# Delta-rule attention and a cosine-gated layer on one core: column steps of units 0 and 1 in one run, 16 constant products, a new order of all work

## The chip, the cores and the metric

The kernel runs on one core of one Trainium2 chip. The metric is the time of one execution on the device in microseconds (us); lower is better. The time before is 648.95 us, the median of three runs (646.66 to 650.49). A change of less than 0.5%, about 3.2 us, can hardly be told from none here.

## What is computed

There are 4 batches with 8 heads, 768 steps in time and a head width of 48. Each head carries a 48 x 48 state. The 8 heads of a token are then joined to a row of 384 numbers, and 3072 such rows go through a gated layer of inner width 2048.

```python
k_n = k / (np.linalg.norm(k, axis=-1, keepdims=True) + 1e-06)
for t in range(S):
    y[:, :, t] = np.einsum('bhd,bhde->bhe', q[:, :, t], state)
    v_old = np.einsum('bhde,bhd->bhe', state, kt)
    state = state + bt[:, :, :, None] * np.einsum('bhd,bhe->bhde', kt, vt - v_old)
...
h = x @ w_in
g = h * np.cos(h)
return (g @ w_out).astype(np.float32)
```

The inputs w_in and w_out come in 8-byte floats and are narrowed on the chip. The state makes the steps in time sequential; the gated layer needs only the finished rows.

## The kernel before

**Units.** The 768 steps are cut into 24 units of 32. Within a unit the steps are coupled by a lower triangular 32 x 32 matrix for each of the 32 batch-head pairs. A unit goes through these tasks, named as in the code: load k, q and v; `turn` and `turn_out` (transposition of k and q by TensorE, copied by ScalarE); `gram` (products of keys with keys and queries, L625); `gram_keys` and `gram_queries` (L639, L748, VectorE); the inverse of the triangle; `state` (L834, keys and queries through the state); `right` (L849); the solve with the inverse; `solve_out` (L907); `update` and `update_out` (L920, L928); `within` (L937); `features` (L956, transposition for the layer). The next unit's `state` needs this unit's `update_out`.

**The inverse.** From unit 4 on, two units (a pair) go through DRAM and are inverted by GpSimd in 31 columns (`invert`, L797 and L804). Units 0 to 3 take another way at the start: the triangle is cut into two blocks of 16 (`fold`, `fold_in`, `fold_off`), the blocks are inverted in 15 column steps, and the coupling between them is done by two more solves (`solve_half`, L864, `between`, L864, `between_out`, L882). A column step is one product on TensorE, which spreads a row of the block over its partitions (`rows`, L707, into one of three PSUM banks with the tag h), and two instructions on the engine that eliminates (`eliminate`: a product at L727, a difference at L734). Step j has a width of x times 15 - j elements, where x is 8 for one unit and 16 for two. GROUPS (L672) says which units go together and ON_POOL (L673) which group is eliminated by GpSimd. Before the change there are three groups: unit 0 alone and unit 1 alone on VectorE, in four tasks each, and units 2 and 3 together on GpSimd, in eight tasks, where ScalarE copies each product out of PSUM first. After a group is done, `unfold` (L742 or L744) puts its inverses where the solves read them.

**The layer.** Two units make a block of 256 rows, a pair p. Pairs 0 and 1 use plain products for the first matrix (`hidden(p, f)`, L980, eight of 24 matmuls by the trace's count), the others a fast scheme with 20 smaller products (`layer`, L1158) of sums of blocks (`x_sum`, L1073). The gate h cos(h) is made by ScalarE and VectorE (`turns` L1021, `rest` L1028, `cos` L1037, `gate` L1040). The second matrix is plain for pair 0 (`output`, L1181) and by seven products for the others (`product`, L1246, with `left_sum` L1262 and `collect` L1298). The weights come in 28 pieces: `narrow_load` on the SP queue, then ScalarE (L497, L499), VectorE (L503, L508) and GpSimd (`narrow_add`, L512, uint32). A `hidden(0, f)` needs 3, 6, 9 or 12 of these additions. Piece 6 and later ones reuse a stage buffer and wait for an addition.

**Constant products.** `heat(width)` (L1194) multiplies a constant with itself into p_out, which nobody reads before the first `output` overwrites it. HEAT (L47) lists the widths; each call becomes two matmul instructions.

**The order.** All work is cut into 2148 tasks with names. LINE (L85) lists their numbers in the order in which they are emitted, and each engine, and SP's queue, runs its own tasks in this order; OTHER (L52) is the set of tasks that go to their second engine (VectorE or GpSimd for sums, ScalarE or VectorE for `fold` and `unfold`). The costs and due times in the code are not read by `add` (L190). An instruction waits by semaphores for what it reads and for the buffers that it writes.

Of the kernel before, what the change touches and what calls it, by code (L numbers as in the profile page):

```python
# [46 lines left out]
HEAT = (512, 256, 256, 512, 128,)  # L47


class Order:  # L50

    OTHER = {  # L52
        ('weigh', 0, 0), ('unfold', 0), ('weigh', 0, 1), ('fold', 1), ('unfold', 1),
        ('weigh', 1, 0), ('fold', 2), ('weigh', 1, 1), ('unfold', 2), ('unfold', 3),
        ('right', 4, 0), ('left', 1, 2, 0), ('x_sum', 2, 'd'), ('x_sum', 2, 'n'),
        ('x_sum', 2, 'm'), ('x_sum', 2, 'e'), ('x_sum', 2, 'k'), ('x_sum', 2, 'g'),
        ('x_sum', 2, 'i'), ('x_sum', 2, 'l'), ('x_sum', 2, 'f'), ('x_sum', 2, 'h'),
        ('x_sum', 2, 'b0'), ('left', 2, 2, 0), ('x_sum', 3, 'd'), ('x_sum', 3, 'n'),
        ('x_sum', 3, 'm'), ('x_sum', 3, 'e'), ('x_sum', 3, 'k'), ('x_sum', 3, 'g'),
        ('x_sum', 3, 'i'), ('x_sum', 3, 'l'), ('x_sum', 3, 'f'), ('x_sum', 3, 'h'),  # L60
        ('x_sum', 3, 'b0'), ('left', 3, 1, 0), ('left', 3, 4, 1), ('left', 3, 3, 0),
        ('x_sum', 4, 'd'), ('x_sum', 4, 'n'), ('x_sum', 4, 'm'), ('x_sum', 4, 'e'),
        ('x_sum', 4, 'k'), ('x_sum', 4, 'g'), ('x_sum', 4, 'l'), ('x_sum', 4, 'f'),
        ('x_sum', 4, 'h'), ('x_sum', 4, 'b0'), ('left', 4, 4, 0), ('left', 4, 3, 0),
        ('left', 4, 3, 1), ('x_sum', 5, 'd'), ('x_sum', 5, 'm'), ('x_sum', 5, 'e'),
        ('x_sum', 5, 'i'), ('x_sum', 5, 'f'), ('x_sum', 5, 'h'), ('left', 5, 2, 0),
        ('left', 5, 4, 0), ('left', 5, 4, 1), ('left', 5, 3, 0), ('x_sum', 6, 'd'),
        ('x_sum', 6, 'e'), ('x_sum', 6, 'l'), ('x_sum', 6, 'f'), ('x_sum', 6, 'h'),
        ('x_sum', 6, 'b0'), ('left', 6, 2, 1), ('left', 6, 4, 0), ('left', 6, 3, 0),
        ('x_sum', 7, 'd'), ('x_sum', 7, 'n'), ('x_sum', 7, 'm'), ('x_sum', 7, 'g'),  # L70
        ('x_sum', 7, 'i'), ('x_sum', 7, 'h'), ('left', 7, 1, 0), ('left', 7, 2, 0),
        ('left', 7, 2, 1), ('left', 7, 4, 0), ('left', 7, 3, 1), ('x_sum', 8, 'd'),
        ('x_sum', 8, 'm'), ('x_sum', 8, 'e'), ('x_sum', 8, 'k'), ('x_sum', 8, 'f'),
        ('x_sum', 8, 'h'), ('x_sum', 8, 'b0'), ('left', 8, 4, 1), ('left', 8, 3, 0),
        ('x_sum', 9, 'n'), ('x_sum', 9, 'e'), ('x_sum', 9, 'k'), ('x_sum', 9, 'i'),
        ('x_sum', 9, 'b0'), ('left', 9, 2, 0), ('left', 9, 1, 1), ('left', 9, 4, 0),
        ('left', 9, 4, 1), ('left', 9, 3, 0), ('left', 9, 3, 1), ('x_sum', 10, 'd'),
        ('x_sum', 10, 'n'), ('x_sum', 10, 'e'), ('x_sum', 10, 'g'), ('x_sum', 10, 'l'),
        ('x_sum', 10, 'f'), ('x_sum', 10, 'h'), ('x_sum', 10, 'b0'), ('left', 10, 1, 0),
        ('left', 10, 1, 1), ('left', 10, 4, 0), ('left', 10, 3, 0), ('x_sum', 11, 'f'),  # L80
        ('x_sum', 11, 'b0'), ('left', 11, 1, 0), ('left', 11, 2, 0), ('left', 11, 2, 1),
        ('left', 11, 4, 0), ('left', 11, 4, 1),
# [139 lines left out]
def kernel(  # L222
# [449 lines left out]
    GROUPS = [(0,), (1,), (2, 3)]  # L672
    ON_POOL = (2,)  # L673
# [1154 lines left out]
```

## Time and profile before

The profiled execution took 644.59 us; its span, from the first to the last instruction, is 642.8 us, so 1.8 us lie around it. It is 0.7% under the median of the three timed runs.

| | us in the profiled execution |
|---|---|
| span | 642.8 |
| TensorE (PE) busy | 613.6 |
| VectorE (DVE) busy | 505.4 |
| GpSimd (POOL) busy | 447.9 |
| ScalarE (ACT) busy | 263.3 |
| first column step of unit 0 (L727) | begins at 15.57 |
| first solve of unit 0 (L864) | begins at 25.36 |
| last column step of unit 1 | begins at 52.46 |
| first product of the layer (L980) | begins at 52.91 |
| first solve of unit 2 (L864) | begins at 81.24 |
| mean granted TensorE clock | 0.981 |

A line of the windows view gives, for a stretch of the span, its length, the busy time and instruction count of PE, of its weight loads (PEld), of DVE, ACT and POOL, then the granted TensorE clock as a share of full speed, the DMA share and GB/s. A line of the timeline gives start, duration, engine, source line, operation, output <- input, shape and count, and in brackets the idle time of the engine before it and what ended it.

### The profile page before, as it was taken

The page shows a single profiled execution, that of the slowest core. Times are in us where ns is not written, and L with a number is a line of the kernel's source. Part 1 is how long each engine was busy: PE and PEld are TensorE (multiplying, and loading weights), DVE is VectorE, ACT ScalarE, POOL GpSimd, SP SyncE. Part 2 cuts the span into 40 slices and gives each one's busy share as a digit, 9 for nine tenths or more (in the row PEclk, how much of TensorE's full clock was granted, in tenths as well). Part 3 has the DMA queues.
Part 4 walks back from the last instruction along what each step waited for, and adds up shares of the span by engine and source line. Part 5 has one row for each costly group of instructions (what it writes and reads, how often), then busy time and mean ns, then how long its engine had stood idle before and what let it go on. Part 6 is the DMA issues. An engine that isn't in the chain of part 4 may idle for free.

```text
span 642.8 us, 28246 instructions
## 1 busy us (share of the span) xinstructions
PE 613.6 (95%) x12316; PEld 572.7 (89%) x12316; DVE 505.4 (79%) x955; ACT 263.3 (41%) x467; POOL 447.9 (70%) x783
## 2 busy tenths in 40 slices
PE   5677999999999999999998999999999999999997
PEld 4566888886999989999998999999999999999997
DVE  7896887599999888789788778777778867556582
ACT  3535565822233631533523533622633433435340
POOL 4465899888888788787888886885897874152032
PEclk9677999999999999999999999999999999999999
DMA  6884475554453542635535404425304202000000
GB/s 122 217 215 133 102 197 140 123 93 70 75 96 51 100 76 40 115 64 99 89 42 98 86 7 84 74 53 101 67 2 85 51 2 34 28 2 26 2 25 25
DMA packets 202924, 50.01 MB, mean 78 GB/s; under 512 B 194544, under 2 KB 197760, under 8 KB 202800
## 3 DMA queue, kind: packets, MB, share of 16 engines
q1 hardware_dynamic: 201536, 47.82, 37.5%
q8 instruction: 97, 1.59, 1.1%
q10 hardware_dynamic: 1088, 0.20, 0.2%
q0 software_dynamic: 176, 0.18, 0.2%
q14 instruction: 27, 0.22, 0.1%
HBM read 38.19 MB, written 9.96 MB: 75 GB/s over the span
## 4 chain that ended last, share of the span: by engine, by line
PE 87%; DVE 7%; DMA 1%; issue 1%; POOL 1%; ACT 1%; SPq 0%; DVEq 0%; POOLq 0%
PE p_out L1246 29%; PE p_h L1158 28%; PE p_h L980 7%; PE p_kq L834 4%; PE p_out L1181 3%; PE p_u L897 3%; PE p_g L625 3%; PE p_s L920 3%; PE p_kq L937 3%; PE p_o L1246 2%; PE p_z L956 1%; DVE rows L734 1%; PE p_t L594 1%; DVE rows L727 1%; DVE g_ffn L1175 1%
## 5 line engine op out<-in xcount | busy, mean ns | idle before, releaser
L797 POOL TENSOR_TENSOR part<-z,gb 128x126 f32<-128x126 f32 (+22 forms) x310 | 138.8, 448 | 39.9 <-DMA gb<-g_dr 7.9
L804 POOL TENSOR_TENSOR z<-z,part 128x126 f32<-128x126 f32 (+22 forms) x310 | 145.8, 470 | 24.3
L1246 PE MATMUL p_out<-w_out,g_ffn 128*128 128x192 f32 x672 | 121.6, 329 | 2.0 <-DVE o L1298 1.8
L1246 PEld LDWEIGHTS p_out<-w_out,g_ffn 128*128 128x128 f32 x672 | 107.8, 190 | 3.7 <-issue 2.2
L1037 ACT ACTIVATE turns<-turns,halfpi 128x512 f32<-128x512 f32 x96 | 68.4, 720 | 78.7 <-DVE turns L1028 78.3
L1262 POOL TENSOR_TENSOR g_ffn<-g_ffn 128x512 f32<-128x512 f32 x37 | 49.0, 1329 | 67.3 <-DVE g_ffn L1040 46.0
L1246 PE MATMUL p_out<-w_sum,g_ffn 128*128 128x192 f32 x496 | 90.1, 329 | 0.4 <-DVE o L1298 0.4
L1158 PE MATMUL p_h<-x_sum,w_in 128*128 128x128 f32 x640 | 83.0, 277 | 0.3 <-DVE g_ffn L1175 0.3
L1246 PEld LDWEIGHTS p_out<-w_sum,g_ffn 128*128 128x128 f32 x496 | 79.5, 190 | 1.4 <-DVE o L1298 0.6
L1158 PEld LDWEIGHTS p_h<-x_sum,w_in 128*128 128x128 f32 x640 | 77.8, 192 | 1.7 <-DVE g_ffn L1175 0.6
L1021 ACT ACTIVATE turns<-g_ffn,quarter_turn 128x512 int32<-128x512 f32 x70 | 49.2, 719 | 59.8 <-DVE g_ffn L1175 38.9
L1175 DVE TENSOR_TENSOR g_ffn<-g_ffn,p_h 128x512 f32<-128x512 f32 x80 | 54.1, 679 | 24.6 <-PE p_h L1158 23.6
L1028 DVE SCALAR_TENSOR_TENSOR turns<-g_ffn,turns 128x512 f32<-128x512 f32 x70 | 55.8, 805 | 15.1 <-ACT turns L1021 14.9
L1040 DVE TENSOR_TENSOR g_ffn<-turns,g_ffn 128x512 f32<-128x512 f32 x70 | 50.9, 736 | 12.7 <-ACT turns L1037 12.6
L1158 PE MATMUL p_h<-x_sum,in_sum 128*128 128x128 f32 x400 | 54.0, 278 | 0.3 <-issue 0.3
L1158 PEld LDWEIGHTS p_h<-x_sum,in_sum 128*128 128x128 f32 x400 | 49.3, 191 | 1.5 <-issue 0.4
L980 PE MATMUL p_h<-x_ffn,w_in 128*128 128x128 f32 x384 | 48.3, 285 | 0.0
L980 PEld LDWEIGHTS p_h<-x_ffn,w_in 128*128 128x128 f32 x384 | 45.7, 198 | 1.0 <-issue 0.2
L1262 DVE TENSOR_TENSOR g_ffn<-g_ffn 128x512 f32<-128x512 f32 x51 | 44.3, 872 | 1.6 <-PE p_out L1246 1.5
L541 POOL TENSOR_TENSOR knrm<-ksum,halves 128x16 f32<-128x16 f32 (+1 forms) x14 | 38.8, 2768 | 9.0 <-DVE ksum L529 7.9
L1298 DVE SCALAR_TENSOR_TENSOR o<-p_out,o 128x192 f32<-128x192 f32 x74 | 25.0, 350 | 24.5 <-PE p_out L1246 23.8
L1170 ACT COPY p_h<-p_h 128x512 f32<-128x512 f32 x40 | 23.0, 574 | 48.9 <-PE p_h L1158 33.6
(145 smaller groups left out, 1052.9 us busy)
## 6 DMA issues: line engine op xcount, KB each, us to landing
gb<-g_dr SPq DMA_DIRECT2D x20, 256.0 KB, 4.1
vp<-in_v_dram SPq DMA_DIRECT2D x96, 48.0 KB, 3.0
in_sum<-in_moe_w_out_dram SPq DMA_DIRECT2D x12, 384.0 KB, 3.3
out_dram<-o SPq DMA_DIRECT2D x23, 192.0 KB, 2.5
in_sum<-in_moe_w_in_dram SPq DMA_DIRECT2D x8, 512.0 KB, 5.3
kp<-in_k_dram SPq DMA_DIRECT2D x128, 24.0 KB, 2.2
z_dr<-z SPq DMA_DIRECT2D x10, 256.0 KB, 3.6
zt<-z_dr SPq DMA_DIRECT2D x80, 32.0 KB, 2.4
```

The lines of the kernel that those rows point to most:

```text
L541: nc.gpsimd.tensor_tensor(out=scales[m][2][:, part], in0=sums[m, part.start][:, 0:n], in1=halves[:, 0:n], op=ALU.pow,)
L797: nc.gpsimd.tensor_tensor(out=part, in0=z[:, 0:rows, j, None].to_broadcast(shape), in1=a[:, j, None, j + 1 :].to_broadcast(shape), op=ALU. ...
L804: nc.gpsimd.tensor_tensor(out=behind, in0=behind, in1=part, op=ALU.subtract)
L980: nc.tensor.matmul(p_h[:, i], w_in[:, t, (4 * k + i) * 128 : (4 * k + i + 1) * 128], xts[p][:, t, unit * 128 : (unit + 1) * 128], start=(i ...
L1021: nc.scalar.activation(turns[p, f], hidden_of(p, f), AF.Identity, bias=quarter_turn, scale=TURN)
L1028: nc.vector.scalar_tensor_tensor(out=r, in0=hidden_of(p, f), scalar=TURN, in1=t, op0=ALU.mult, op1=ALU.subtract,)
L1037: nc.scalar.activation(r, r, AF.Sin, bias=halfpi, scale=2.0 * math.pi)
L1040: nc.vector.tensor_tensor(out=place(p, f), in0=step_of(rests.pop((p, f)), f), in1=step_of(hidden_of(p, f), f), op=ALU.mult,)
L1158: nc.tensor.matmul(p_h[:, e], in_block(*w)[:, e], x_of(p, b), start=new and e == 0, stop=True, skip_group_check=True,)
L1175: nc.vector.tensor_tensor(out=part_of(p, to), in0=part_of(p, one), in1=part_of(p, two), op=op)
L1246: nc.tensor.matmul(p_o, left(p, part, a)[:, e % 4], right(e, b), start=(e == 0), stop=(e == FT // 2 - 1), skip_group_check=True,)
L1262: either(("left", p, x, s), nc.vector, nc.gpsimd).tensor_tensor(out=left(p, s, to), in0=left(p, s, one), in1=left(p, s, two), op=op)
```

## The change

1. GROUPS becomes [(0, 1), (2, 3)] and ON_POOL (1,). Units 0 and 1 are eliminated together by VectorE in eight tasks of two columns each, with widths from 240 down to 16 in place of twice 120 down to 8. There are 15 fewer products on TensorE and 30 fewer instructions on VectorE. Unit 0's solves now wait for unit 1's triangle as well.
2. HEAT has 16 entries in place of 5.
3. OTHER and LINE are new: 2158 tasks. By count, `unfold` of units 0 to 3 moves from ScalarE to VectorE (4 tasks), `weigh` moves from GpSimd to VectorE for 3 of 4 tasks, 5 `x_sum` and one each of `in_sums` and `right` move to GpSimd, 2 `left` and one `fold` move to VectorE.

```diff
-HEAT = (512, 256, 256, 512, 128,)
+HEAT = (128, 256, 256, 512, 512, 128, 128, 256, 256, 128, 512, 256, 128, 256, 512, 128,)
...
-    GROUPS = [(0,), (1,), (2, 3)]
-    ON_POOL = (2,)
+    GROUPS = [(0, 1), (2, 3)]
+    ON_POOL = (1,)
```

The numbers of LINE say little by themselves, so here are the first tasks of the two engines that matter most, by name, in the old and the new order (unit or group first, then the step):

```
TensorE, old: turn 0; heat; turn 1; gram 0; gram 1; rows 0,0; turn 2; rows 0,1; rows 0,2; rows 0,3; turn 3;
 rows 1,2; rows 1,0; solve_half 0; between 0; heat; solve 0; rows 1,1; update 0; within 0; heat; turn 4;
 state 1; features 0; rows 1,3; gram 2; heat; gram 3; hidden 0,0; rows 2,0; solve_half 1; rows 2,1;
 between 1; rows 2,2; rows 2,4; solve 1; heat; rows 2,3; update 1; within 1; turn 5; hidden 0,2; ...
TensorE, new: heat; turn 0; heat; heat; turn 1; gram 0; gram 1; heat; rows 0,0; rows 0,1; heat; rows 0,4;
 rows 0,2; turn 2; rows 0,3; heat; rows 0,5; heat; heat; rows 0,7; turn 3; rows 0,6; heat; heat; heat; heat;
 solve_half 0; between 0; heat; solve 0; heat; update 0; within 0; turn 4; state 1; features 0; gram 2;
 hidden 0,0; gram 3; heat; solve_half 1; rows 1,0; between 1; rows 1,1; rows 1,3; solve 1; rows 1,2; update 1;
 within 1; turn 5; rows 1,5; rows 1,6; rows 1,4; features 1; state 2; gram 4; hidden 0,2; gram 5; rows 1,7;
 hidden 0,8; solve_half 2; ...
VectorE, old: sum 0; picks; picks; beta; sum; scale 0; scale; spread 0; gram_keys 0; fold 0; fold_in 0; sum 1;
 gram_keys 1; gram_queries 1; gram_queries 0; begin_rows; eliminate 0,0 to 0,1; fold_in 1; eliminate 0,2 to 0,3;
 shift 0; scale 1; sum 1; shift 1; begin_rows; shift 2; scale 1; between_out 0; eliminate 1,0; solve_out 0;
 shift 3; sum 2; shift 4; update_out 0; shift 5; eliminate 1,1; shift 6; eliminate 1,2; gram_keys 2; ...
VectorE, new: sum 0; sum; beta; picks; picks; scale; scale 0; gram_keys 0; fold 0; fold_in 0; gram_keys 1;
 fold 1; fold_in 1; gram_queries 1; begin_rows; gram_queries 0; spread 0; eliminate 0,0 to 0,7; unfold 0;
 sum 1; shift 0; sum 1; between_out 0; shift 1; solve_out 0; sum 2; update_out 0; scale 1; shift 2; spread 1;
 unfold 1; scale 1; shift 4; spread; gram_keys 2; shift 3; weigh; gram_queries 2; right 1; spread; shift 5;
 fold_in 2; gram_keys 3; gram_queries 3; fold 3; fold_in 3; shift 6; rest 0,0; between_out 1; ...
```

The two DVE instructions of a piece of weights are called shift here, the GpSimd addition add. GpSimd's new head is: weigh; norms of units 2 and 3 (two tasks, L541); add 0; add 1; norms of the next pair; add 2; add 4; add 3; add 5; begin_rows; add 6; eliminate 1,0 to 1,7; add 7; add 8; add 10; add 9; norms; add 11; add 12; the first inverse of the long way. In the old head two additions (10 and 8) stand within the eight eliminations and the inverse follows add 13.

More of the change, by code (lines that the diff above doesn't have):

```diff
@@ L44, in _consts @@
     ).astype(np.float32)
-HEAT = (512, 256, 256, 512, 128,)
+HEAT = (128, 256, 256, 512, 512, 128, 128, 256, 256, 128, 512, 256, 128, 256, 512, 128,)
 class Order:
     OTHER = {
[L53 to L61, printed above, removed]
-        ('x_sum', 4, 'd'), ('x_sum', 4, 'n'), ('x_sum', 4, 'm'), ('x_sum', 4, 'e'),
[L63 to L82, printed above, removed]
@@ new lines @@
+        ('weigh', 0, 0), ('fold', 2), ('right', 3, 2), ('right', 4, 4), ('left', 1, 1, 1),
+        ('in_sums', 17), ('x_sum', 2, 'd'), ('x_sum', 2, 'n'), ('x_sum', 2, 'm'),
[4 rows of a table added]
+        ('x_sum', 3, 'f'), ('x_sum', 3, 'h'), ('x_sum', 3, 'b0'), ('left', 3, 3, 1),
+        ('x_sum', 4, 'd'), ('x_sum', 4, 'n'), ('x_sum', 4, 'm'), ('x_sum', 4, 'e'),
+        ('x_sum', 4, 'i'), ('x_sum', 4, 'l'), ('x_sum', 4, 'f'), ('left', 4, 4, 0),
+        ('left', 4, 4, 1), ('left', 4, 3, 0), ('left', 4, 3, 1), ('x_sum', 5, 'd'),
@@ new lines @@
+        ('x_sum', 5, 'n'), ('x_sum', 5, 'm'), ('x_sum', 5, 'g'), ('x_sum', 5, 'l'),
+        ('x_sum', 5, 'f'), ('left', 5, 1, 1), ('left', 5, 2, 1), ('left', 5, 4, 0),
+        ('left', 5, 4, 1), ('left', 5, 3, 0), ('left', 5, 3, 1), ('x_sum', 6, 'd'),
+        ('x_sum', 6, 'm'), ('x_sum', 6, 'e'), ('x_sum', 6, 'k'), ('x_sum', 6, 'g'),
+        ('x_sum', 6, 'i'), ('x_sum', 6, 'l'), ('x_sum', 6, 'f'), ('x_sum', 6, 'b0'),
+        ('left', 6, 2, 0), ('left', 6, 4, 1), ('left', 6, 3, 0), ('x_sum', 7, 'd'),
@@ new lines @@
+        ('x_sum', 7, 'i'), ('x_sum', 7, 'l'), ('x_sum', 7, 'h'), ('x_sum', 7, 'b0'),
+        ('left', 7, 1, 0), ('left', 7, 2, 0), ('left', 7, 3, 0), ('left', 7, 3, 1),
+        ('x_sum', 8, 'd'), ('x_sum', 8, 'n'), ('x_sum', 8, 'k'), ('x_sum', 8, 'g'),
+        ('x_sum', 8, 'l'), ('x_sum', 8, 'b0'), ('left', 8, 1, 1), ('left', 8, 2, 1),
+        ('left', 8, 3, 0), ('left', 8, 3, 1), ('x_sum', 9, 'm'), ('x_sum', 9, 'e'),
+        ('x_sum', 9, 'k'), ('x_sum', 9, 'g'), ('x_sum', 9, 'f'), ('x_sum', 9, 'h'),
@@ L83 @@
+        ('left', 9, 1, 1), ('left', 9, 4, 1), ('left', 9, 3, 0), ('x_sum', 10, 'e'),
+        ('x_sum', 10, 'k'), ('x_sum', 10, 'h'), ('left', 10, 1, 0), ('left', 10, 2, 0),
+        ('left', 10, 2, 1), ('left', 10, 4, 1), ('left', 10, 3, 0), ('x_sum', 11, 'e'),
+        ('x_sum', 11, 'f'), ('x_sum', 11, 'h'), ('left', 11, 2, 0), ('left', 11, 2, 1),
+        ('left', 11, 4, 1), ('left', 11, 3, 0),
     }
     LINE = """
[98 rows of a table removed]
[98 rows of a table added]
 """
```

200 rows, old and new, of tables (LINE, OTHER) are left out of this document.

## The prediction

> **What bounds the kernel now.** I read the page's busy line first, then the windows view cut by stage, then the chain of waits, then the timeline of the first 82 us.
>
> ```profile
> PE 613.6 (95%) x12316; PEld 572.7 (89%) x12316; DVE 505.4 (79%) x955; ACT 263.3 (41%) x467; POOL 447.9 (70%) x783
> ```
>
> This is the share of busy time over the whole span. By stage (the stretch, its length, then busy time and count of PE, PEld, DVE, ACT and POOL, the granted clock, DMA share, GB/s):
>
> ```profile
> 0.00:12.00 12.00, 5.87 (x47) 4.06 (x51) 8.88 (x28) 4.11 (x8) 6.79 (x12) 1.00 0.68 108
> 12.00:22.00 10.00, 8.07 (x175) 7.27 (x158) 8.41 (x34) 3.86 (x8) 0.00 (x0) 1.00 0.81 202
> 22.00:30.00 8.00, 5.73 (x138) 4.64 (x138) 6.30 (x20) 6.10 (x13) 5.49 (x4) 0.52 0.86 215
> 30.00:40.00 10.00, 6.39 (x170) 5.71 (x170) 9.66 (x20) 4.51 (x9) 5.26 (x5) 0.53 0.92 267
> 40.00:53.00 13.00, 7.44 (x278) 5.51 (x277) 11.98 (x30) 3.71 (x9) 8.89 (x7) 0.87 0.79 197
> ...
> 82.00:140.00 58.00, 56.65 (x1290) 49.23 (x1278) 46.47 (x84) 34.12 (x67) 49.46 (x89) 1.00 0.62 149
> 140.00:200.00 60.00, 59.76 (x1374) 51.99 (x1374) 58.73 (x106) 16.24 (x29) 52.27 (x92) 1.00 0.46 75
> ...
> 300.00:400.00 100.00, 97.71 (x1990) 93.33 (x1988) 81.19 (x142) 40.03 (x68) 79.83 (x149) 1.00 0.42 73
> ```
>
> From 82 us on PE is full: idle 1.35, 0.24 and 2.29 us in the three late rows shown. TensorE bounds the kernel there, and its work there is the same after the change. In the first 53 us it idles 6.13 + 1.93 + 2.27 + 3.61 + 5.56 = 19.5 us, and from 22 to 40 us it has half its clock (the 0.52 and 0.53). So the question is how much earlier the steady part starts. VectorE is what ends the waits in the start: the chain runs through L727 and L734 from 15.5 to 23.1 us and again from 42.6 to 51.6.
>
> ```profile
> 25.36 1.50 PE L864 MATMUL p_w<-vp,halves_z 32*32 32x48 f32 x64 [1.59 <-issue]
> ...
> 33.77 1.50 PE L897 MATMUL p_u<-u_half,halves_z 32*32 32x48 f32 x64 [3.61 <-DVE u_half L882]
> ...
> 51.64 1.34 PE L625 MATMUL p_g<-kq_t 48*32 48x64 f32 x64 [4.31 <-DVE rows L727]
> 52.91 4.66 PE L980 MATMUL p_h<-x_ffn,w_in 128*128 128x128 f32 x24
> ```
>
> Between 25 and 53 us PE waits 3.6 us for VectorE's L882, which stands behind a `scale`, and 4.3 us for the column steps of unit 1, which VectorE does between weight shifts. The 4.66 us of the last row is 2.9 at full clock (later rows of L980).
>
> **The column steps.** Three rows of VectorE give a law:
>
> ```profile
> 12.74 0.42 DVE L639 TENSOR_TENSOR rows<-p_g,bs 128x256 f32<-128x256 f32 x1 [0.61 <-PE p_g L625]
> ...
> 15.57 0.28 DVE L727 TENSOR_TENSOR rows<-rows,p_r 128x120 f32<-128x120 f32 x1
> ...
> 23.17 0.17 DVE L727 TENSOR_TENSOR rows<-rows,p_r 128x8 f32<-128x8 f32 x1
> ```
>
> From 8 to 120 elements the time grows by 0.11 us, 0.98 ns an element; at 256 the law gives 0.41, measured 0.42. The fixed part is 0.16, and 0.03 lies between two. A group of 8 costs 30 x 0.19 + 2 x 960 x 0.00098 = 7.6 us (the row of unit 0: 15.57 to 23.6, with one other instruction within). The double group costs 5.7 + 3.8 = 9.5 us against 15.2 for two, so 5.7 less. Unit 1's steps also ran beside POOL's additions, where a difference at L734 of 0.21 us took 1.27, 1.02 and 0.50; some 3 us of that goes too. Against it VectorE takes over `unfold` (4 x 0.6 from the 0.28 of a tensor_scalar, twice) and three `weigh` (0.55 each): 4.0 us.
>
> **The path through the start, step by step, with before's durations** (before's times in brackets):
> - `gram_keys` 0 at 13.4 (12.74). VectorE now waits for the second norm sum at 8.94 before it makes the picks: 8.94 + 0.55 + 0.49 (beta) + 1.68 (picks) + 2 x 0.85 (scales).
> - First column step at 17.1 (15.57): two units' keys and folds (2 x 1.15), two `gram_queries` (0.74), begin 0.4, spread 0.2.
> - Last step ends at 27.7: 9.5, and 1.0 for PE, where turn 2 (1.23), turn 3 and three heats stand before the rows of steps 3 and 6. `unfold` 0.6: 28.3 (25.25).
> - `solve_half` 0 at 29.4 (25.36): the four heats before it take 0.70 + 0.49 + 1.13 + 0.70 from 26.4, so 1.0 us of them lies on the path. Unit 0 is 4 us late here.
> - `between_out` at 31.8 (33.17). At full clock 0.88, 0.5 and 0.88 lie between. VectorE has only two sums and a shift before it, 2.2 us, and no `scale` that waits for POOL.
> - `solve_out` at 33.5 (35.93), `update_out` ends at 36.4 (41.64; it stood behind two shifts and a sum), turn 4, state 1 (1.31), features, gram 2: PE starts `hidden` at 40.4 (52.91). That needs add 2, for which I find POOL free at 38.7, done at 40.0.
> - Unit 1: VectorE still has four shifts, a `weigh` and two `gram_keys`. I let six POOL additions of 1.28 us cost it 3 us in all. `gram_queries` 2 at 46.0 frees the bank for gram 3, 3 frees it at 50 for `solve_half` 1 (58.31). Solves, update, turn 5 and three rows bring `hidden` 0,2 to 64.4 (67.9).
> - POOL eliminates from 53.2 (59.2). Before's stretch of 20.0 us holds 3.2 of additions, so 16.8: 70.0 (79.2). With `unfold`, `solve_half` 2 stands at 71.6 (81.24), and PE has two more `gram` and two `hidden` to fill until 71.3.
>
> By 81.24 the old order had done four `hidden`, by 71.6 the new one three: 9.7 - 2.9 = **6.8 us ahead**.
>
> **The heats.** At full clock a heat of 512, 256 and 128 takes 1.13, 0.70 and 0.49 (L1194), so the 16 cost 4 x 1.13 + 6 x 0.70 + 6 x 0.49 = 11.7 us, the five of before 5.5. All but the 1.0 above lie in idle PE time; without that cover they cost 6.2 us. What they are worth is the clock. Before, it fell at 22.8 us though PE was idle for only 1.2 us from 16 to 22: its work there was transpositions and rows of 8 to 88 columns. At half clock the solves took 1.50 for 0.88, update 1.56 for 0.89, `hidden` 4.66 for 2.9. I count all at full clock: in the new order PE is busy from 13 to 30 us, with wider rows and nine heats in it.
> The Trainium skill (TensorE: Matmul & The Clock Gate, The HAM clock gate) has the clock halved after an idle window of about 3.4 us. No such gap precedes 22.8 in the trace; by its rule the new order, whose longest gap I put at 2.8 us, stays warm, by the row it need not.
>
> **Later.** Moves between engines change VectorE by -1.8 us and POOL by +2.7 over 560 us (5 x_sum at 0.42 and 0.59, 2 left at 0.87 and 1.33, a right, an in_sums): nothing while both idle over 20% of it. From 140 to 200 us VectorE is 98% full, so a lead holds there only if its work comes earlier as well; it does by the walk, since its units are ahead. SP's queue: v 0 goes 0.3 us later, under the column steps; v 1 stands behind piece 6, which waits for add 0 (34.3), lands at 40, needed at 44. The wait for the three banks of `rows` is in the 1.0 above.
>
> The sum against the profiled execution is 644.6 - 6.8 = 637.8; the same off the median of 648.95 is **642.0**.
>
> **The rivals.**
> - *More than that.* If POOL's additions cost VectorE nothing and the heats end with the steps, the lead is 6.8 + 3 + 1 = 11, and if the late idle of 5.6 us (82 to 640 us) shrinks too, 14: 635 to 639. For it: the new order leaves several us more PE work between an inverse and its solve. Chance 0.22.
> - *The clock falls all the same*, as at 22.8. PE's 4.1 us of rows, turns and heats from 22.2 to 26.3 take 1.7 times that, the heats too: 5 us late, and a lead of 2: 647. Or the double width costs double (0.56 in place of 0.40 at 240): 15.2 us, lead 1. Against it: the 0.42 row. Or the lead is lost in the full VectorE of 140 to 200. Chance 0.22 together, all within 0.5%.
> - *Slower.* The new order lets VectorE's bursts reach PE in the steady part. Before shows one: from 288.8 to 300.9 the chain runs on VectorE, and PE idles 1.67 us in that pair of units (300 to 350 us). If each of ten pairs pays that, it is 16.7 for the 5.6 of today: 11.1 more, less the lead of 6.8: 653.3. It decides from 1.0 us a pair more than today's 0.56. Against it: counted in the two orders, 163 PE tasks of the old one and 161 of the new stand less than 1 us of PE work behind the task that they wait for. Chance 0.18.
> - *As forecast*, 638.5 to 645.7: 0.38.
>
> **The numbers.** Faster by over 0.5% (0.5% is 3.2 us, about what can be told from no change): 0.38 + 0.22 = 0.60; within 0.5%: 0.22; slower: 0.18. The range for 8 in 10 is 633 to 654: its low end takes in most of the first rival, its high end that of the bursts.
>
> **What would show it.** Right: L727 on VectorE as 15 instructions of 0.40 down to 0.17 from about 17 to 27.5 us; a clock of 1.00 from 22 to 40; `solve_half` 0 near 29.4 and the first L980 near 40; `solve_half` 2 near 71.6; PE idle after 82 us near 6. Wrong: PE late at 29 with a halved clock; L882 or L928 behind shifts again; PE idle of over 10 us after 82 us with VectorE as releaser.

## The result, and the profile after

The changed kernel takes 658.55 us, median of four runs (656.10 to 666.83), the kernel before 649.43 beside it. The ratio is 1.0134, 95% interval 1.0085 to 1.0183: 1.3% slower, where 642.0 us and "faster" were forecast. One of the four runs, 666.83, was disturbed and is left out of the ratio. The profiled execution took 658.11 us with a span of 655.9.

The page's busy line, then the windows view by the stretches of before:

```profile
PE 618.7 (94%) x12308; PEld 574.1 (88%) x12308; DVE 495.5 (76%) x931; ACT 261.0 (40%) x458; POOL 438.2 (67%) x785
```

```profile
22.00:30.00 8.00, 5.81 (x137) 4.29 (x139) 6.82 (x23) 5.36 (x11) 2.60 (x2) 1.00 0.66 140
30.00:40.00 10.00, 8.34 (x246) 6.49 (x235) 6.06 (x15) 2.11 (x5) 7.26 (x5) 0.66 0.81 245
40.00:53.00 13.00, 9.81 (x364) 7.79 (x361) 10.37 (x27) 8.21 (x17) 7.04 (x6) 1.00 0.53 127
...
82.00:140.00 58.00, 55.24 (x1182) 49.53 (x1171) 45.55 (x85) 33.53 (x64) 46.91 (x81) 1.00 0.62 142
140.00:200.00 60.00, 55.93 (x1238) 46.11 (x1238) 55.33 (x95) 14.81 (x27) 50.64 (x94) 1.00 0.44 72
...
500.00:600.00 100.00, 96.93 (x1613) 93.41 (x1612) 68.40 (x115) 40.23 (x69) 51.51 (x91) 1.00 0.14 30
```

The last of these rows in the kernel before:

```profile
500.00:600.00 100.00, 99.97 (x1641) 96.70 (x1641) 66.26 (x119) 40.28 (x70) 47.02 (x84) 1.00 0.09 20
```

The start is better: full clock at 22 to 30 us, and from 30 to 53 us VectorE (the third busy time) is busy for 16.4 of 23 us, before for 21.6. The late rows are worse. Length less PE's busy time is PE's idle time: 2.76, 4.07 and 3.07 us here, against 1.35, 0.24 and 0.03 before; from 82 to 600 us it is 14.7 against 5.1. Of the 14.7 the trace puts 9.2 us to waits for VectorE, 2.6 to waits for ScalarE and 2.5 to stops without a releaser.

The timeline, at the steps that the prediction walked (lines of the changed file are three lower: L727 is L724, L864 is L861, L980 is L977):

```profile
16.55 0.40 DVE L724 TENSOR_TENSOR rows<-rows,p_r 128x240 f32<-128x240 f32 x1 [0.19 <-PE p_r L704]
...
27.94 0.88 PE L861 MATMUL p_w<-vp,halves_z 32*32 32x48 f32 x64 [1.48 <-DVE halves_z L741]
...
31.93 0.32 PE L861 MATMUL p_v<-u_half,halves_z 32*32 32x48 f32 x2 [1.58 <-issue]
...
42.10 0.67 PE L831 MATMUL p_kq<-st,kq_t 48*32 48x48 f32 x48 [1.52 <-issue]
...
44.61 1.60 PE L977 MATMUL p_h<-x_ffn,w_in 128*128 128x128 f32 x12
...
76.01 1.44 PE L861 MATMUL p_w<-rhs,halves_z 32*32 32x48 f32 x64 [2.20 <-DVE halves_z L741]
```

The first column step and the first solve stand where the walk put them. Then something new: TensorE stops for 1.5 us in the middle of a run of 64 or 128 equal products, and "issue" says that the profile shows nothing that it waited for. And solve_half 2 comes at 76.0 in place of 71.6.

To see where the lead went I add up TensorE's work in each profiled execution, each product at its usual pace in the kernel before (column and constant products left out, so that all kernels have the same 532 us of work), and take the difference to the kernel before at the same time. Ahead is positive:

| profiled run | 65 us | 110 | 220 | 520 | 600 |
|---|---|---|---|---|---|
| changed kernel | 3.3 | 0.8 | -7.5 | -9.0 | -11.8 |
| e2, old start, new rest | -0.1 | -0.1 | -7.7 | -9.0 | -11.8 |
| e3, new to 230 us | 2.7 | 0.2 | -12.0 | -12.7 | -13.9 |
| p4, new start mended, old rest | 1.5 | 1.9 | -1.3 | -1.5 | -2.0 |
| f1, eight waits taken away | 3.4 | 3.7 | -3.8 | -6.3 | -7.5 |
| p3, f1 with a mended start | 5.0 | 7.0 | -0.9 | -7.4 | -8.6 |
| q1, p3 without twelve sums | 5.6 | 7.1 | 4.8 | 1.8 | 1.2 |
| g, single columns | 0.7 | -3.9 | -12.5 | -14.4 | -18.0 |
| e5b, nine products narrow | 0.7 | -5.3 | -14.9 | -17.4 | -21.8 |

The changed kernel is 3.3 us ahead at 65 us, level at 100, and loses 8 us from 110 to 220 and 3 from 520 to 600. The table is worked out from one execution of each, which need not be a typical one: q1's took 644.68 us, the least of its ten, whose median is 651.13. The ratios below are from timed runs.

### The profile page after: what moved, and what is told of

Its sections match the earlier page's. It is cut to its first block, busy times and chain, and to the rows that moved or that the text cites. A ratio compares the mean times of both kernels' runs of the same rounds, so it can differ in the third digit from the quotient of the medians.

```text
span 655.9 us, 28183 instructions
## 1 busy us (share of the span) xinstructions
PE 618.7 (94%) x12308; PEld 574.1 (88%) x12308; DVE 495.5 (76%) x931; ACT 261.0 (40%) x458; POOL 438.2 (67%) x785
## 4 chain that ended last, share of the span: by engine, by line
PE 66%; DVE 17%; SPq 4%; issue 3%; DMA 2%; ACT 2%; POOL 0%; DVEq 0%; ACTq 0%; POOLq 0%
PE p_out L1243 22%; PE p_h L1155 21%; PE p_h L977 6%; PE p_kq L831 3%; DVE turns L1025 3%; PE p_s L917 3%; PE p_u L894 2%; PE p_g L622 2%; PE p_kq L934 2%; SPq L354 2%; DVE g_ffn L1037 2%; DVE g_ffn L1172 2%; PE p_out L1178 2%; DVE x_sum L1070 1%; DVE g_ffn L1259 1%
## 5 line engine op out<-in xcount | busy, mean ns | idle before, releaser
L794 POOL TENSOR_TENSOR part<-z,gb 128x126 f32<-128x126 f32 (+22 forms) x310 | 141.5, 456 | 52.5 <-DMA gb<-g_dr 10.4
L801 POOL TENSOR_TENSOR z<-z,part 128x126 f32<-128x126 f32 (+22 forms) x310 | 135.8, 438 | 24.3
L1259 POOL TENSOR_TENSOR g_ffn<-g_ffn 128x512 f32<-128x512 f32 x35 | 47.5, 1364 | 77.9 <-DVE g_ffn L1259 34.6
L1172 DVE TENSOR_TENSOR g_ffn<-g_ffn,p_h 128x512 f32<-128x512 f32 x80 | 54.3, 679 | 16.7 <-PE p_h L1155 16.6
L1037 DVE TENSOR_TENSOR g_ffn<-turns,g_ffn 128x512 f32<-128x512 f32 x70 | 51.8, 743 | 12.8 <-ACT turns L1034 12.7
L1155 PE MATMUL p_h<-x_sum,in_sum 128*128 128x128 f32 x400 | 53.4, 278 | 0.0
L977 PE MATMUL p_h<-x_ffn,w_in 128*128 128x128 f32 x384 | 49.4, 288 | 1.3 <-issue 1.1
L977 PEld LDWEIGHTS p_h<-x_ffn,w_in 128*128 128x128 f32 x384 | 46.7, 201 | 2.8 <-issue 1.2
L538 POOL TENSOR_TENSOR knrm<-ksum,halves 128x16 f32<-128x16 f32 (+1 forms) x14 | 37.0, 2642 | 13.0 <-DVE ksum L526 13.0
L1155 PE MATMUL p_h<-x_ffn,w_in 128*128 128x128 f32 x320 | 42.3, 278 | 0.8 <-ACT p_h L1167 0.8
```

Source lines behind the costliest of these rows:

```text
L538: nc.gpsimd.tensor_tensor(out=scales[m][2][:, part], in0=sums[m, part.start][:, 0:n], in1=halves[:, 0:n], op=ALU.pow,)
L794: nc.gpsimd.tensor_tensor(out=part, in0=z[:, 0:rows, j, None].to_broadcast(shape), in1=a[:, j, None, j + 1 :].to_broadcast(shape), op=ALU. ...
L801: nc.gpsimd.tensor_tensor(out=behind, in0=behind, in1=part, op=ALU.subtract)
L977: nc.tensor.matmul(p_h[:, i], w_in[:, t, (4 * k + i) * 128 : (4 * k + i + 1) * 128], xts[p][:, t, unit * 128 : (unit + 1) * 128], start=(i ...
L1037: nc.vector.tensor_tensor(out=place(p, f), in0=step_of(rests.pop((p, f)), f), in1=step_of(hidden_of(p, f), f), op=ALU.mult,)
L1155: nc.tensor.matmul(p_h[:, e], in_block(*w)[:, e], x_of(p, b), start=new and e == 0, stop=True, skip_group_check=True,)
```

## The experiments

All times are medians, each ratio is to the kernel before, run beside it:

| run | us | ratio, 95% interval |
|---|---|---|
| e1 new start, old rest | 650.45 | 1.0044, 1.0007 to 1.0082 |
| e2 old start, new rest | 661.36 | 1.0212, 1.0159 to 1.0264 |
| e3 new to 230 us, old rest | 659.11 | 1.0178, 1.0144 to 1.0212 |
| e4 old to 230 us, new rest | 659.48 | 1.0176, 1.0123 to 1.0229 |
| e5 without nine constant products | 668.52 | 1.0301, 1.0234 to 1.0368 |
| e5b those nine narrowed | 667.18 | 1.0297, 1.0241 to 1.0353 |
| s128 before, half a block later | 692.99 | 1.0721, 1.0658 to 1.0784 |
| s256 before, a whole block later | 647.82 | 1.0024, 0.9994 to 1.0053 |
| f1 eight waits taken away | 657.13 | 1.0177, 1.0105 to 1.0249 |
| f2 f1, last rows early | 656.20 | 1.0161, 1.0095 to 1.0227 |
| g single columns | 664.68 | 1.0312, 1.0235 to 1.0388 |
| h before, 11 more constant products | 646.24 | 1.0005, 0.9969 to 1.0042 |
| p1 e1, edges restored | 648.83 | 1.0027, 0.9996 to 1.0058 |
| p2 changed kernel, 16 instructions more | 663.82 | 1.0248, 1.0185 to 1.0311 |
| p3 f2, 16 instructions more | 657.81 | 1.0182, 1.0116 to 1.0248 |
| p4 p1, start mended | 646.30 | 0.9992, 0.9962 to 1.0021 |
| q1 p3 without twelve sums | 651.13 | 1.0028, 0.9997 to 1.0058 |
| q2 before without twelve sums | 646.74 | 0.9972, 0.9954 to 0.9990 |

**Which part loses (e1 to e4).** LINE of one kernel up to a point, the remaining numbers in the order of the other; each task keeps the engine that its order gave it.

```diff
-LINE = the 2158 numbers of the changed kernel
+LINE = its first 406 (e1) or 734 (e3), then the rest as in the kernel before
-LINE = the 2148 numbers of the kernel before
+LINE = its first 391 (e2) or 759 (e4), then the rest as in the changed kernel
```

> The changed kernel up to the products of unit 6 (its first 406 of 2158 pieces of work, to about 125 us), and from there all work in the order and with the engine choices of the kernel before. Theory (the start is a gain or neutral, and the 9 us are lost by the new order of the steady part, from 100 us on): by the curve of TensorE's work done, the changed kernel stands about 1 to 3 us ahead at this seam, so 646 to 649 us, with TensorE idle under 8 us from 140 to 640 us. Rival (the start itself loses, by its half-clock stretches and its gaps without a releaser): 654 to 660 us, near the changed kernel's 658.

> The mirror image: the kernel before up to about 110 us (its first 391 of 2148 pieces of work), then the changed kernel's order and engine choices. Theory (the steady part's new order loses): 656 to 661 us, with TensorE idle over 9 us from 140 to 640 us. Rival (the start loses): 648 to 651 us.

> As the first, with the seam later: the changed kernel's order up to the first product of the output layer of pair 2 (734 pieces of work, about 230 us), then the order of the kernel before. Theory (most of the steady part's loss lies between 125 and 300 us, by the curve about 6 of 9 us before 230): 652 to 656 us, that is 4 to 8 us above the run with the early seam. Rival (the loss lies in the last third, after 500 us, where the changed kernel's TensorE idles 3 us more): within 2 us of the early seam.

> The kernel before up to about 230 us (its first 759 pieces of work), then the order and the engine choices of the changed kernel. With the seam at 110 us the new rest cost 14.6 us. Theory (the waits of 0.5 to 1.5 us between 130 and 215 us, which that run has at the same places as the changed kernel, are 7 to 9 us of it, and the last third the rest): 651 to 655 us. Rival (all of it lies behind 230 us, or grows out of the seam itself): 659 to 662 us.

The loss is in the rest: 2.1% with the old start (e2), and the new start with the old rest stays within 0.8% of the kernel before. e3 against e1 puts 1.3% between 125 and 230 us. e1 came out between its theory and its rival, 0.4% slower where a gain or nothing was expected: the start brings nothing to the end. e2 and e3 came out 0.4 and 3.1 us above their theories. e4 came out as its rival, so the parts don't add up: its trace has 4.1 us of waits at 231.5, 233.9 and 314.9 us, of which e2's has 0.4.

**The stops without a releaser (s128, s256).** On the changed kernel's page, among the DMA queues (packets, MB, share):

```profile
q8 instruction: 96, 1.57, 1.0%
```

That is 16,384 bytes a packet, and 12308 products with their weight loads make 24,616 instructions, 256 a packet. Counted in TensorE's instructions (with the 158 that are neither), the seven such gaps of the changed kernel come at 705, 1218, 1473, 2497, 10690, 11714 and 13250, the two of the kernel before at 2754 and 15809: multiples of 256 apart, to within one. At four of those edges in the changed kernel:

| edge | edge before passed | packet starts, lands | TensorE goes on | gap |
|---|---|---|---|---|
| 705 | 26.08 | 29.52, 30.79 | 31.93 | 1.58 |
| 1217 | 37.66 | 39.76, 40.78 | 42.10 | 1.52 |
| 1473 | 42.10 | 44.73, 45.94 | 47.31 | 1.10 |
| 2497 | 58.93 | 62.04, 63.02 | 64.34 | 1.53 |

So the next block of code was late. The test moves the edges and nothing else:

```diff
-HEAT = (512, 256, 256, 512, 128,)
+HEAT = (512, 256, 256, 512, 128,) + (16,) * 32    # s256: * 64
+        if width < 128: product of 32x32 by width columns, and return
-LINE = 92 0 1 ...
+LINE = the 32 (64) new tasks, then 92 0 1 ...
```

> The kernel before, unchanged but for 32 tiny constant products (32x32 by 16 columns, 128 TensorE instructions) ahead of all its work, where TensorE idles until 7.9 us. New theory, from the traces so far: TensorE's instructions come by DMA in packets of 16,384 bytes (256 instructions, queue q8), one is asked for when about 50 instructions of the block before it are left, and it is usable about 3.2 to 4 us later; where 256 instructions pass faster than that, in stretches of narrow products, TensorE stands still at the block's edge, with no releaser in the trace. So the time hangs on where the edges fall in the work. In the kernel before they fall well: 0.98 us of such gaps. Moved by half a block, the same work should meet about 13 gaps of 1 to 2.5 us, one for each second unit, near 79, 124, 169, 218, 258, 299, 346, 377, 402, 454 and 501 us: 660 to 672 us. Rival (the gaps without a releaser have nothing to do with blocks): within 2 us of the kernel before.

> The control: 64 tiny products (256 instructions) ahead of the kernel before, so that the edges of the blocks fall on the same work as in the kernel before, one block later. Theory of the block edges: within 2 us of the kernel before, though it has twice as many products as the run with half a block. Rival (added products cost, whatever the edges): as far off as the run with half a block, or further.

Half a block costs 46 us, a whole block, with twice the added products, next to nothing. The timeline of s128:

```profile
82.16 0.65 PE L626 MATMUL p_g<-kq_t 48*32 48x64 f32 x22 [3.37 <-issue]
...
134.47 0.53 PE L835 MATMUL p_kq<-st,kq_t 48*32 48x48 f32 x20 [2.95 <-issue]
```

Such stops stand at 24 edges and make 40 us. Of the twenty over 0.15 us, ten lie exactly 1024 instructions, four blocks, behind another: the work of a unit comes round about that often, so a bad place repeats. Summed in the same way, the steps at edges that waited for their packet are 3.4 us in the kernel before, 2.1 in s256 and 10.7 in the changed kernel, 7.3 of these before 82 us. The theory holds, and the cost, 46 us, is about twice the most that I had put (25 us): the stops are more and longer than the 13 that I counted, and the clock goes down with them (73 us at half clock in s128, 24 in the kernel before).

**The clock (e5, e5b, h).** e5 leaves nine constant products out, e5b makes them 16 columns wide (their instructions stay), h adds 11 wide ones to the kernel before.

```diff
-HEAT = (128, 256, 256, 512, 512, 128, 128, 256, 256, 128, 512, 256, 128, 256, 512, 128,)
+HEAT = (128, 256, 256, 16, 16, 16, 16, 16, 16, 16, 16, 16, 128, 256, 512, 128,)    # e5b
```

> The changed kernel without nine of its sixteen constant products, those between the products of unit 1 and solve_half 0 (13.6 to 26.1 us, 7.5 us of TensorE). Theory (they hold the clock, and the clock is worth time at the start only): the granted clock falls to 0.5 near 22 us as in the kernel before, solve_half 0 starts within 0.5 us of 27.9, the chain from there to the first hidden products is 2 to 5 us longer, and the whole kernel takes 659 to 662 us. Rival (they are worth nothing, or stand in the way): 656 to 658.5 us.

> The changed kernel with nine of its sixteen constant products (those between 13.6 and 26.1 us) narrowed to tiny ones: their busy time is gone, their 36 instructions stay, so the block edges stay on the same work. Leaving them out cost 10 us. Theory (about 7 us of that came from the block edges, which moved by 36 instructions, and the rest from the clock, which fell at 18 us): 660 to 664 us, the clock falling near 20 us again. Rival (all of it is the clock): 667 to 670 us.

> The kernel before with 11 more constant products of 256 and 512 columns in the idle times of TensorE between 18 and 52 us, and 53 tiny ones ahead of all work, so that the 64 add one whole block and the edges stay on the same work after that. This is the part of the change that is to hold the clock, alone. Theory (in the kernel before VectorE is busy 96 of 100 us from 30 to 40 us and 92 of 100 from 40 to 53, so a full clock saves TensorE's own steps on the path only, at most 2.5 us): clock 1.00 from 22 to 40 us, 644 to 647 us. Rival (as in the changed kernel, where nine such products are worth 9 us): 638 to 642 us.

e5 came out dearer than both its theory and its rival. My theory of e5b fell: with the edges in place the loss is the same (1.0297 against 1.0134, some 10 us), so the nine products are worth 10 us by their busy time. Without them the clock is at half for 41 us of the profiled run, with them for 14, and TensorE is 5.3 us behind at 110 us in place of 0.8 ahead. In the old order the same help is worth nothing (h), though it worked:

```profile
22.00:30.00 8.00, 7.34 (x164) 6.12 (x162) 7.20 (x28) 5.06 (x11) 4.98 (x4) 1.00 0.90 214
30.00:40.00 10.00, 6.03 (x163) 4.86 (x164) 9.65 (x19) 5.46 (x9) 5.26 (x5) 0.75 0.95 288
```

The clock is 1.00 and 0.75 for 0.52 and 0.53, and VectorE is at 9.65 of 10 us as before. So I take it that VectorE sets the pace there.

**The doubling (g).** The eight doubled steps become four of unit 0 and four of unit 1, in turn:

```diff
-    GROUPS = [(0, 1), (2, 3)]
-    ON_POOL = (1,)
+    GROUPS = [(0,), (1,), (2, 3)]
+    ON_POOL = (2,)
+LINE: eliminate (0, s) of the changed order becomes (s % 2, s // 2), rows alike; 49 tiny products first
```

> The changed order with the column steps of units 0 and 1 as in the kernel before: two groups of four steps of four columns each, which take the places of the eight doubled steps in turn; 49 tiny products ahead of all work keep the block edges on the same work (256 instructions in all with the column products that this adds). This takes the doubling alone away. Theory of the prediction (9.5 us for the doubled steps and 15.2 us for the single ones): solve_half 0 comes 5 to 6 us later, at 33 to 34 us, and the whole kernel takes 662 to 665 us. Rival (what the start gains is lost before 100 us whatever it is): 657 to 660 us.

```profile
16.58 0.27 DVE L726 TENSOR_TENSOR rows<-rows,p_r 128x120 f32<-128x120 f32 x1
...
33.72 1.04 PE L863 MATMUL p_w<-vp,halves_z 32*32 32x48 f32 x64
```

solve_half 0 at 33.7, 5.8 us later, as the law of the column steps gives. At the end the kernel is 6.4 us of span and 1.8% by ratio slower than the changed one. In the new order the doubling is worth what was forecast or more; the rival falls.

**The waits of the rest (f1, f2, p2, p3).** Behind 82 us TensorE's largest waits look like this (timeline of the changed kernel):

```profile
156.39 0.87 DVE L1117 TENSOR_TENSOR in_sum<-in_sum,w_in 128x512 f32<-128x512 f32 x1
...
159.74 0.90 DVE L1117 TENSOR_TENSOR w_in<-w_in 128x512 f32<-128x512 f32 x1
...
160.56 1.01 DVE L904 TENSOR_TENSOR u<-p_u,bz 128x384 f32<-128x384 f32 x2
...
161.72 0.89 PE L917 MATMUL p_s<-u,kp 64*64 64x96 f32 x32 [1.49 <-DVE u L904]
```

Five sums of weights stand ahead of solve_out 5 on VectorE, and TensorE's update waits 1.5 us. e2 has the same wait, 1.49 us at 161.96, so it belongs to the order. f1 moves eight such tasks in LINE; f2 moves the last column products of units 2 and 3 too; p2 and p3 put 16 instructions ahead.

```diff
-in_sums 11; in_sums 13; in_sums 3; in_sums 16; features_out 4; solve 5; out 0,1,3; solve_out 5
+features_out 4; solve 5; out 0,1,3; solve_out 5; in_sums 11; in_sums 13; in_sums 3; in_sums 16   # f1, and seven more
-hidden 0,2; split 10; rows_copy 1,5; shift 7; gram 5; ...; rows 1,7
+rows 1,7; split 10; rows_copy 1,5; hidden 0,2; shift 7; gram 5   # f2, with unfold 2 on ScalarE
```

> The changed kernel with eight pieces of VectorE's or ScalarE's work put earlier or later in the order, where TensorE waited for them behind a burst: solve_out 2 (89.6 us, 0.9), features_out 3 (119.4 us, 1.6), solve_out 5 ahead of four sums of weights (161.7 us, 1.5), gram_queries 8 ahead of the sums of tokens (172.0 us, 0.5), a left product of pair 1 (183.4 us, 1.0), layer_out 34 of pair 2 (212.7 us, 1.0) and the two collects of pairs 7 and 8 (505.5 and 548.0 us, 1.3 and 1.6). TensorE's own order, and so its block edges, stay. Theory (these waits of 9.4 us are the steady part's loss): 649 to 652 us. Rival (the work put back makes TensorE wait elsewhere, one wait for another): 655 to 659 us.

> As the run f1, and in the start the last column products of units 2 and 3 ahead of a group of hidden products, with unfold 2 on ScalarE: GpSimd waited 3.3 us for these at 70.9 us, and solve_half 2 came at 76.0 us, after a gap of 2.2 us and with the clock falling to a half. Theory (that wait is on the path and costs the clock too): GpSimd done by 70 us, solve_half 2 near 72 us, 2 to 4 us less than f1. Rival (TensorE has other work there): within 1 us of f1.

> The changed kernel with four tiny products (16 TensorE instructions) ahead of all work: it has 16 TensorE instructions fewer than the kernel before, so this puts the edges of the late blocks back. By the same sum the shortfall is 14.7 us in the changed kernel and 12.3 us with this shift. Theory (the edges are a small part of the changed kernel's loss): a ratio to the kernel before of 1.007 to 1.011 where the changed kernel has 1.0134, 2 to 4 us better. Rivals: (the edges are all of it) 1.000 to 1.003; (16 instructions do nothing) 1.012 to 1.015.

> The run f2 (the changed kernel with eight waits taken away and the last column products early) with the same four tiny products ahead. Theory (the waits taken away came back as gaps at block edges): 650 to 653 us, with under 2 us of gaps without a releaser behind 82 us. Rival (they came back as other waits): 655 to 657 us as f2.

f1 came out as its rival: it gains nothing that its interval can tell. Its profiled run is 4.2 us of span shorter, of 9.4 us of waits. The timeline shows what came in their place:

```profile
156.56 0.89 PE L917 MATMUL p_s<-u,kp 64*64 64x96 f32 x32
...
163.97 0.83 PE L622 MATMUL p_g<-kq_t 48*32 48x64 f32 x61 [0.87 <-issue]
```

The update no longer waits, and TensorE gets to its next block edge too soon. f2, too, came out as its rival: GpSimd still waits 4.0 us for rows, and solve_half 2 starts at 76.6 us. p2 refutes all three of its theories: 16 instructions made the changed kernel 1.1% slower, not faster. I have no cause for that. p3 stays at f2's time, but its start is what the prediction walked, solve_half 2 at 70.47 us,

```profile
70.47 0.88 PE L861 MATMUL p_w<-rhs,halves_z 32*32 32x48 f32 x64 [0.33 <-ACT halves_z L739]
```

and it holds 7.0 us of lead at 110 us, to lose 15.6 us from there to 600. So neither the start nor these eight waits account for the loss. p3 came out near its rival, and its 14.8 us of waits from 82 to 600 us are others: 4.6 for VectorE, 3.9 for the DMA of the inverses, 3.4 for ScalarE, 2.8 without a releaser.

**The start with the old rest (p1, p4).** e1 with 28 instructions ahead, which brings the late edges near their place in the kernel before; p4 mends the start as f2 does.

```diff
+LINE = seven tiny products, then e1's order          # p1
+ rows 1,7 ahead of hidden 0,2; solve_out 2 and features_out 3 earlier; unfold 2 on ScalarE   # p4
```

> The run e1 (new start to 125 us, old order behind it) with seven tiny products (28 TensorE instructions) ahead of all work, which put the block edges of the rest within a few instructions of where the kernel before has them. Summed over the blocks behind 80 us, the work of a block at its usual pace falls short of 3.4 us by 14.3 us in e1, by 8.2 us with this shift, by 8.5 us in the kernel before. Theory (the start's lead of 1 to 3 us at the seam was eaten by worse edges behind it): 643 to 647 us where e1 had 650 and the kernel before 646.8. Rival (the lead is already gone at the seam): 649 to 651 us.

> The run p1 with the last column products early, unfold 2 on ScalarE, and solve_out 2 and features_out 3 ahead of the work that kept them (all of it before 125 us). Theory (the start's own waits were worth 2 to 4 us): 640 to 644 us, faster than both kernels. Rival (TensorE's time there is set by its blocks' supply): as p1, within 1.5 us.

p1 came out between its theory and its rival. p4 missed its theory: mended in every way I found, the new start equals the old one (0.9992). Its 1.9 us of lead at 110 us is -0.7 at 120; 1.4 us of that is one stop at a block edge, at 117.99 us.

The traces show what VectorE meets next. In p4 it runs from 125 to 205 us with pauses of 0.6 us at the most; some 18 of these 80 us are the 22 sums of weights (`in_sums`). The first of them needs GpSimd's addition 24, which is the 24th of 28 in the old order and the last in the new. It ends at 130.7 us in the kernel before, at 138.5 in the changed kernel. There VectorE waits for it, and then twice for TensorE:

```profile
138.51 0.69 DVE L1117 TENSOR_TENSOR in_sum<-w_in 128x512 f32<-128x512 f32 x1 [2.51 <-POOL w_out L509]
142.24 1.02 DVE L904 TENSOR_TENSOR u<-p_u,bz 128x384 f32<-128x384 f32 x2 [3.04 <-PE p_u L894]
...
145.94 0.95 DVE L925 TENSOR_TENSOR st<-st,p_s 128x768 f32<-128x768 f32 x1 [1.61 <-PE p_s L917]
```

The first two of these steps in the kernel before, in the other order and without a wait:

```profile
138.01 1.00 DVE L907 TENSOR_TENSOR u<-p_u,bz 128x384 f32<-128x384 f32 x2
...
139.97 0.77 DVE L1120 TENSOR_TENSOR in_sum<-w_in 128x512 f32<-128x512 f32 x1
```

From 128 to 148 us VectorE stands still for 7.2 us in the changed kernel, 9.0 in e2, 7.6 in f1 and 8.2 in p3, but for 0.4 in the kernel before and 0.7 in p4. Late additions alone are not the cause: in p3 addition 24 ends at 130.9 us, as early as before, and the first sum starts 9 us earlier than before, yet VectorE stands still and 7.9 us of lead are lost from 110 to 220 us.

**VectorE as the bound (q1, q2).**

```diff
     def in_sums(i):
+        if i >= 10:
+            return
```

> The run p3 without the last twelve of the 22 sums of weights (numbers 10 to 21, which change blocks of the weights in place; eleven of them on VectorE, some 9 us between 150 and 210 us); the weights that follow are then other numbers. Theory (VectorE sets the pace there and eats the 7 us of lead): TensorE keeps its lead to 220 us, and the kernel takes 648 to 652 us, 6 to 9 less than p3. Rival (the new order's own sequence sets it, whatever VectorE has to do): 655 to 658 us.

> The kernel before without the same twelve sums (all on VectorE, some 10 us). There TensorE is busy 59.8 of 60 us from 140 to 200 us. Theory (in the kernel before VectorE and TensorE are both full there, so the shorter of the two doesn't help): 644.5 to 647 us. Rival (VectorE alone is the bound, in both): 636 to 640 us.

Without some 9 us of VectorE's work q1 is 1.5% faster than p3, some 10 us; the kernel before gains 0.3%, 1.8 us. Both times lie where their theories put them. The windows view of 140 to 200 us, first p3, then q1, then q2:

```profile
140.00:200.00 60.00, 56.41 (x1254) 47.89 (x1255) 58.02 (x100) 16.19 (x29) 51.93 (x89) 1.00 0.44 71
```

```profile
140.00:200.00 60.00, 59.35 (x1466) 52.05 (x1464) 54.70 (x99) 18.19 (x32) 49.15 (x92) 1.00 0.46 73
```

```profile
140.00:200.00 60.00, 60.00 (x1374) 51.75 (x1374) 50.92 (x94) 16.53 (x30) 51.50 (x99) 1.00 0.46 75
```

In p3 VectorE is full and TensorE idles 3.6 us; with the sums gone TensorE idles 0.65 us, and q1 keeps 4.8 of its 7.1 us to 220 us. In the kernel before both were full already. A rival would be that TensorE no longer waits for the sums themselves; but in p3 no wait of TensorE from 110 to 220 us is put down to a sum. q1 still has the 7.6 us in which VectorE stands still, so less work makes up for them; no run took away these waits alone.

## Why the prediction was wrong

- *The column steps*: right. The first instruction, 240 wide, takes 0.40 us, the last ends at 27.2 (27.7 said), and g shows that they are worth what was put on them.
- *The path through the start*: right to solve_half 0 (27.9 for 29.4) and again for solve_half 1 (50.6 for 50) and GpSimd's begin (53.4 for 53.2). Three terms were missed: block edges (5.7 us in four gaps from 31 to 65 us), the clock, at half from 31.8 to 38.6, 65.9 to 69.3 and 76.1 to 79.6 us where I counted it full, and 3.25 us that GpSimd waited for its last rows, which stood behind hidden 0,2 on TensorE. The lead at 80 us was 0.6, not 6.8. p3, with those rows early and 16 instructions ahead, has 6.8; f2, the same without the 16, has 1.7. A slip of the sum is small: 648.95 less 6.8 is 642.15, not 642.0.
- *The heats*: their place in idle time was right, their worth far too small: 10 us in the new order, nothing in the old. Before, the clock's record falls at 22.4 us, not at 22.8.
- *"Later", nothing is lost*: this is the step that failed. Behind 110 us the kernels of the table with the new rest and all of its work lose 11 to 17 us, whatever their lead (f2, which is not in it, 9). I wrote that a lead holds through the full VectorE of 140 to 200 us "only if its work comes earlier as well; it does by the walk, since its units are ahead". VectorE's work there did not come earlier with the units. The last sum of weights ends at 195.4 us before, at 211.0 in the changed kernel and at 204.9 in p3, though p3 was 7 us ahead at 110. Just ahead of that stretch VectorE stands still for 7.2 us (8.2 in p3) where before it stood still for 0.4, and in the stretch it has no slack to make that up. That the amount of VectorE's work decides is shown by q1, for p3; that these waits are what uses it up is argued from the traces. The count of tasks close behind what they wait for was no test of this, since it has no durations of the other engines in it.
- *The slower rival* named the engine rightly: 9.2 of TensorE's 14.7 idle us from 82 to 600 us are waits for VectorE. That its 16.7 us came near is in part luck: it spread them evenly, 1.67 us for each of ten pairs, while the measured lead falls by 8.3 us from 110 to 220 us, by 1.5 from there to 520 and by 2.8 in the last 80. It still credited 6.8 us of lead, which were gone, so it said 653 for 658.

What stays open: why p2 is slower, and how the 11 to 17 us divide between VectorE's waits, its order and the block edges. No version that does all of the work beat the kernel before by more than its interval; p4 is level with it.

## What to carry to other kernels

A start that is shortened pays only if every engine that is full later is relieved with it: before counting a lead, follow what the next full engine works on in that stretch back to its own inputs, and look for its waits just ahead of it. In a stream of narrow products look at each stop without a releaser and count the instructions up to it; if the counts differ by one fixed number, the supply of code sets the pace, and a few instructions more or less anywhere ahead can move the time by more than the change under study. So a comparison of two orders needs a control with the edges put back in place.

## What the runs showed of the hardware

- **Code comes in blocks of 256 instructions.** In the twenty traces no packet starts earlier than 0.74 us behind the point 48 instructions ahead of the edge before; it takes 0.88 us at least, and 1.03 us at least pass until the first instruction. In the first 82 us, where the DMA share of the changed kernel is 0.52 to 0.91, the packet starts on average 1.7 us after the edge before (where it starts behind it), later 1.2. A run of 32x48 products takes 14 ns for a product and its load, so 256 instructions pass in 1.8 us. The Trainium skill (Runtime: NRT & Kernel Launch, Terms) has the instruction memory refilled in 16 KiB blocks; the packets agree, and what that costs a kernel is measured here (46 us for half a block).
- **The clock falls after windows that are about half idle.** In the twenty traces it goes down behind 80 us 23 times, in steps of 3.41 us, and in the 3.41 us before each fall TensorE idled 1.38 us or more. Of 3284 such windows without a fall eight idled over 1.5 us. The Trainium skill (TensorE: Matmul & The Clock Gate, The HAM clock gate) speaks of an idle window of about 3.4 us; the length agrees, but in 16 of the 23 falls 1.4 to 2 us of idling in it were enough.
